# First block's weight loads regrouped over three issuing engines in a fused MLP forward and backward kernel

## The chip, the cores and the metric

The kernel runs on one core of one Trainium2 chip. The metric is the device time of one execution in microseconds, the median of several executions: 271.76 us before the change (three runs, 271.73 to 272.64). A core has a matrix engine (TensorE, PE in the profile, with weight loads listed as PEld), three engines for elementwise work (VectorE or DVE, ScalarE or ACT, GpSimd or POOL) and SyncE (SP), which here only issues transfers. Transfers are carried out by 16 DMA engines, which all queues of the core share. SP, ACT and POOL each have a queue of their own; an issuing instruction occupies its engine for some tenths of a microsecond up to several microseconds, and the data land later.

## The reference

A two-layer MLP with the tanh form of GELU, and its gradients, in bf16:

```python
B, S, D, F = 1, 2048, 448, 1792
h = jnp.einsum("bsd,df->bsf", x, w1) + b1
h = jax.nn.gelu(h, approximate=True)
out = jnp.einsum("bsf,fd->bsd", h, w2) + b2
# outputs: out and the gradients of x, w1, b1, w2, b2 for a given grad_out
```

## The kernel before, in words

The 2048 rows are worked in four blocks of 512 (`NB`, `SB`); the block that is worked first holds rows 512 to 1023. Inside a block the 1792 columns of the hidden layer are worked in seven pairs of 128-column tiles (`NPAIR`), in the order of `FP = [1, 2, 3, 4, 5, 6, 0]`. So pair 0 of a block reads columns 256 to 511 of w1, pair 1 columns 512 to 767, pair 2 columns 768 to 1023, pair 3 columns 1024 to 1279, and pair 6 columns 0 to 255.

For each pair the order, written out by hand under a manual schedule, is:

- `pe_u_fulls` (line 216): u = x·w1 with three matmuls of 128 rows of w1 (`w1_f`) per tile.
- `pe_tails` (line 237): the last 64 rows. 448 is three times 128 plus 64, and the 64 left-over rows of w1 stand in a tile of their own, `wt1` (the profile calls it wt). The left-over half of q, read from `w2T`, is worked beside it on the other 64 rows of the array. The two halves are issued alternately: u, q, u, q.
- `pe_q_fulls` (line 273): q = grad_out·w2ᵀ, from the transposed weight `w2T` and the transposed gradient `gT`.
- `copy_u` (line 311, with one line 313 on DVE), `act_gelu` (317), `act_square` (320), `act_tanh` (329) on ACT; `dve_cubic`, `dve_gate` and `dve_gh` (324 to 343) on DVE. They make `hT`, the activation, and `ghT`, the gradient before the first layer.
- `pieces` (line 372): the matmuls of the second layer, first with `w2_sb` and `hT`, and from pair 6 on with `w1T_sb` and `ghT` for the gradient of x.

u runs two pairs ahead of q. The numbers in brackets below, u(3) or q(1), count pairs through all blocks, and `pieces` behind q(1) needs hT(1).

In the first block all weights arrive from memory while the matmuls already run. SP issues nearly all of these loads in one order, written out at lines 142 to 168; ACT issues the first piece of w1, and POOL the bias b1. `load_w1` (lines 121 and 122) issues two transfers, the 384 full rows of a column range into `w1_f` and the 64 left-over rows of the same range into `wt1`. `load_w2` (line 125) loads row tiles of w2 into `w2_sb`. `load_w2T` (lines 129 to 133) loads w2 transposed, for columns 0 to 255 in two transposes and one 2 KB copy of 64 by 16 single elements (line 133). `load_g` (line 114) and `load_x` (line 104) are transposing loads of one block. Line 167 loads the whole of w1 transposed into `w1T_sb`. Plain and transposing loads go through the same SP queue in that order. In the compiled program the loads of SP and ACT take eight landing counters in turn, so that a load waits for the landing of the eighth load before it.

At the start 42 dummy matmuls (line 172) run on PE until x arrives. After the four blocks come the weight gradients (lines 662, 673, 694), which work on data held or reloaded by then.

Of the kernel before, what the change touches and what calls it, by code (L numbers as in the profile page):

```python
# [19 lines left out]
def kernel(  # L20
# [15 lines left out]
    nc = tc.nc  # L36
    P = 128
    B, S, D = x.shape
    F = w1.shape[1]
    assert (B, S, D, F) == (1, 2048, 448, 1792)  # L40
    NS = S // P
    NF = F // P
    KF = D // P
    DL = D - KF * P
    SB = 512
# [8 lines left out]
    ROW0 = [SB, 2 * SB, 3 * SB, 0]  # L54
# [4 lines left out]
    x2 = x.rearrange("b s d -> (b s) d")  # L59
# [21 lines left out]
    w2T = const.tile([P, KF + 1, F], BF16, name="w2T")  # L81
# [13 lines left out]
    xT, gT = {}, {}  # L95

    def wide(src, r0, n, shift):
        return bass.AP(src.tensor, src.offset + r0 * D - shift, [[D, n], [1, (KF + 1) * P]])
# [11 lines left out]
    def load_g(b):  # L110
        t = blk.tile([P, KF + 1, SB], BF16, name="gT", tag="gT")
        r0 = ROW0[b]
        if b in WIDE:
            nc.sync.dma_start_transpose(out=t[:], in_=wide(g2, r0, SB, DL))  # L114
        else:
            nc.sync.dma_start_transpose(out=t[:, 1:KF + 1, :], in_=g2[r0:r0 + SB, DL:D])
            nc.sync.dma_start_transpose(out=t[:, 0, :], in_=g2[r0:r0 + SB, 0:P])
        gT[b] = t

    def load_w1(eng, f0, f1):  # L120
        eng.dma_start(out=w1_f[:, :, f0:f1], in_=w1[0:KF * P, f0:f1].rearrange("(kt p) f -> p kt f", p=P))  # L121
        eng.dma_start(out=wt1[0:DL, f0:f1], in_=w1[KF * P:D, f0:f1])  # L122

    def load_w2(eng, t0, t1):
        eng.dma_start(out=w2_sb[:, t0:t1, :], in_=w2[t0 * P:t1 * P, :].rearrange("(ft p) d -> p ft d", p=P))  # L125

    def load_w2T(f0, f1):
        if f0 > 0:
            nc.sync.dma_start_transpose(out=w2T[:, :, f0:f1], in_=wide(w2, f0, f1 - f0, DL))  # L129
        else:  # L130
            nc.sync.dma_start_transpose(out=w2T[:, :, 16:f1], in_=wide(w2, 16, f1 - 16, DL))
            nc.sync.dma_start_transpose(out=w2T[:, 1:KF + 1, 0:16], in_=w2[0:16, DL:D])
            nc.sync.dma_start(out=w2T[DL:P, 0, 0:16], in_=w2[0:16, 0:DL].rearrange("f d -> d f"))

    nc.vector.memset(zero[:], 0.0)
    nc.gpsimd.memset(b1_rows[:], 0.0)
# [2 lines left out]
    nc.gpsimd.dma_start(out=b1_rows[0:NF, :], in_=b1.rearrange("(ft p) -> ft p", p=P))  # L139
    xT[0] = blk.tile([P, KF + 1, SB], BF16, name="xT", tag="xT")  # L140
    halves = [slice(0, SB // 2), slice(SB // 2, SB)]
    nc.sync.dma_start_transpose(out=xT[0][:, :, halves[0]], in_=wide(x2, ROW0[0], SB // 2, 0))
    load_w1(nc.scalar, 256, 512)
    nc.sync.dma_start_transpose(out=xT[0][:, :, halves[1]], in_=wide(x2, ROW0[0] + SB // 2, SB // 2, 0))
    warm = stg.tile([P, 1], F32, name="warm", tag="warm", bufs=1)
    nc.scalar.activation(out=warm[:], in_=zero[:, 0:1], func=ACT.Gelu_apprx_tanh)
    load_w1(nc.sync, 512, 768)
    load_w1(nc.sync, 768, 1024)
    load_w2(nc.sync, 2, 4)
    load_g(0)  # L150
    load_w2T(256, 512)
    load_w2(nc.sync, 4, 6)
    load_w1(nc.sync, 1024, 1280)
    load_w2T(512, 768)
    load_w2(nc.sync, 6, 8)
    load_w1(nc.sync, 1280, 1536)
    load_w2T(768, 1280)
    load_w2(nc.sync, 8, 12)
    load_w1(nc.sync, 1536, F)
    load_w1(nc.sync, 0, 256)  # L160
    load_w2(nc.sync, 12, NF)
    load_w2(nc.sync, 0, 2)
    load_w2T(1280, F)
    nc.sync.dma_start(out=b2_bc[:], in_=b2.rearrange("(o d) -> o d", o=1).to_broadcast((P, D)))
    load_x(1)
    load_w2T(0, 256)
# [257 lines left out]
    loads = {6: ("x", 2), 8: ("g", 2), 10: ("x", 3), 11: ("g", 3)}  # L424
# [44 lines left out]
    for i in range(1, NSINGLE):  # L469
        f = i + LEAD  # L470
# [271 lines left out]
```

## Time and profile before

| what | value |
|---|---|
| median of three runs | 271.76 us |
| the profiled execution: its own time | 272.33 us |
| its span, first to last instruction | 270.5 us |
| PE busy in the span | 263.7 us (97%) |
| DVE / ACT / POOL busy | 176.1 / 139.3 / 39.7 us |
| first matmul on real data | 5.64 us |
| w1T_sb: issued, landed | 34.54 us, 46.01 us |
| granted TensorE clock | 1.000 |

The span is counted from the first instruction on; 1.8 us of the execution's own time lie around it, and that execution is 0.57 us above the median of the runs. PE is busy nearly all the time, so that time can only be won or lost where PE stands still. It does so in a few places, which the list of waits and the timeline of PE give one by one. In the DMA part of the page the queue q1 is SP's, q10 ACT's and q0 POOL's; q8 and q14 are transfers of instructions. "Us to landing" counts from the start of the issuing instruction to the landing of the data.

### The profile page before, as it was taken

The numbers are of one execution on the slowest core, as the hardware profiler recorded it, in microseconds if no ns is written. First come the engines' busy times: TensorE is split into PE (matmuls) and PEld (weight loads), VectorE is DVE, ScalarE is ACT, GpSimd is POOL, SyncE is SP. The second block draws the span as 40 slices with busy tenths as digits, with TensorE's granted clock in tenths as the row PEclk, the third lists the DMA queues.
The fourth block names the chain that finished last, engine by engine and source line by source line (L and its number), as shares of the span: only waits on it lengthen the run. The fifth ranks groups of instructions, "written<-read, shape, count | busy, mean of one in ns | idle before, by whom it ended". The sixth has DMA issues, their size and how long they took to land.

```text
span 270.5 us, 4721 instructions
## 1 busy us (share of the span) xinstructions
PE 263.7 (97%) x1941; PEld 148.0 (55%) x1948; DVE 176.1 (65%) x208; ACT 139.3 (51%) x163; POOL 39.7 (15%) x50
## 2 busy tenths in 40 slices
PE   8999998999999999999999999999999999999995
PEld 7334343444445665555457888874444665555554
DVE  1689999799999779696798930309999992000000
ACT  2898899689995867968676520012111211111111
POOL 1000004011002020110202021221510007900000
PEclk9999999999999999999999999999999999999999
DMA  7999989999999995162642439999311111999851
GB/s 161 207 186 252 180 168 186 252 261 183 250 257 218 266 210 130 61 166 58 168 101 93 78 56 249 368 242 271 92 40 39 41 29 45 195 224 227 202 126 34
DMA packets 112965, 44.44 MB, mean 164 GB/s; under 512 B 92032, under 2 KB 111824, under 8 KB 112944
## 3 DMA queue, kind: packets, MB, share of 16 engines
q1 hardware_dynamic: 106352, 36.43, 63.2%
q0 software_dynamic: 1824, 4.27, 5.2%
q10 hardware_dynamic: 4768, 3.44, 4.1%
q8 instruction: 15, 0.25, 0.4%
q14 instruction: 6, 0.05, 0.1%
HBM read 7.23 MB, written 14.23 MB: 79 GB/s over the span
## 4 chain that ended last, share of the span: by engine, by line
PE 82%; SPq 12%; DMA 4%; issue 1%; ACT 0%
PE ps L237 23%; PE ps_v L694 16%; PE ps_w L662 13%; PE pq L237 9%; PE pu L237 8%; DMA w1T_sb<-in_w_dram 4%; PE ps L372 4%; SPq L129 4%; PE pu L216 3%; PE pq L273 2%; PE ps_w L673 2%; SPq L125 1%; SPq L104 1%; SPq L121 1%; SPq L122 1%; SPq L114 1%
## 5 line engine op out<-in xcount | busy, mean ns | idle before, releaser
L311 ACT ACTIVATE U<-pu,b1T 128x512 bf16<-128x512 f32 x55 | 33.9, 687 | 20.3 <-PE pu L237 20.1
L343 DVE SCALAR_TENSOR_TENSOR ghT<-Z,pq 128x1024 bf16<-128x1024 bf16 x28 | 33.9, 1221 | 14.2 <-PE pq L237 11.5
L386 POOL DMA_DIRECT2D out_dram<-st x32 | 19.1, 602 | 161.4 <-ACT st L383 107.6
L694 PE MATMUL ps_v<-g_nat,h_nat 128*128 128x448 bf16 (+1 forms) x240 | 42.6, 340 | 0.0
L237 PE MATMUL pq<-gT,w2T 64*128 64x512 bf16 x242 | 36.2, 376 | 0.6 <-DMA w2T<-in_w_dram 0.5
L662 PE MATMUL ps_w<-gh_nat,x_nat 128*128 128x512 bf16 (+1 forms) x192 | 36.5, 352 | 0.0
L237 PE MATMUL ps<-w1T_sb,ghT 64*128 64x448 bf16 x336 | 33.9, 349 | 0.0
L694 PEld LDWEIGHTS <-h_nat 128*128 128x128 bf16 x240 | 23.3, 98 | 19.3 <-DMA out_dram<-st 0.3
L237 PE MATMUL ps<-w_sb,hT 64*128 64x448 bf16 x336 | 33.7, 349 | 0.0
L329 ACT ACTIVATE Z<-Z 128x2048 bf16<-128x2048 bf16 (+1 forms) x18 | 27.5, 1528 | 7.7 <-DVE Z L325 7.6
L648 DVE TENSOR_TENSOR acc<-acc,gh_nat 128x1792 f32<-128x1792 f32 x14 | 30.0, 2142 | 0.5
L662 PEld LDWEIGHTS <-x_nat 128*128 128x128 bf16 x192 | 18.7, 98 | 17.9 <-issue 0.4
L237 PEld LDWEIGHTS <-ghT 64*128 64x128 bf16 x336 | 23.5, 94 | 8.7
L320 ACT ACTIVATE A<-U 128x1024 bf16<-128x1024 bf16 (+1 forms) x19 | 27.7, 1457 | 0.7 <-DVE U L313 0.4
L317 ACT ACTIVATE hT<-U 128x1024 bf16<-128x1024 bf16 (+1 forms) x20 | 27.7, 1391 | 0.2
L237 PEld LDWEIGHTS <-hT 64*128 64x128 bf16 x336 | 20.4, 94 | 11.9
L697 ACT CAST st<-ps_v 128x448 bf16<-128x448 f32 (+1 forms) x15 | 7.6, 507 | 34.8 <-PE ps_v L694 34.8
L383 ACT CAST st<-ps 128x448 bf16<-128x448 f32 x20 | 9.8, 532 | 29.0 <-PE ps L237 27.6
L216 PE MATMUL pu<-xT,w_f 128*128 128x512 bf16 (+1 forms) x100 | 22.6, 366 | 0.6 <-DMA xT<-in_x_dram 0.4
L237 PEld LDWEIGHTS <-w2T 64*128 64x128 bf16 x248 | 18.0, 94 | 8.7 <-DMA w2T<-in_w_dram 1.1
L665 ACT CAST st<-ps_w 128x512 bf16<-128x512 f32 (+1 forms) x12 | 6.4, 533 | 28.9 <-PE ps_w L662 28.9
L237 PE MATMUL pu<-xT,w_f 64*128 64x512 bf16 x144 | 20.5, 376 | 0.0
(52 smaller groups left out, 256.0 us busy)
## 6 DMA issues: line engine op xcount, KB each, us to landing
hT_dram<-hT SPq DMA_DIRECT2D x28, 256.0 KB, 3.0
out_dram<-st POOLq DMA_DIRECT2D x32, 112.0 KB, 3.5
x_nat<-in_x_dram SPq DMA_DIRECT2D x1, 1792.0 KB, 9.5
g_nat<-in_grad_out_dram SPq DMA_DIRECT2D x1, 1792.0 KB, 14.4
out_dram<-st ACTq DMA_DIRECT2D x13, 112.0 KB, 3.4
w_f<-in_w_dram SPq DMA_DIRECT2D x6, 192.0 KB, 4.1
out_dram<-st ACTq DMA_DIRECT2D x9, 128.0 KB, 1.7
w_sb<-in_w_dram SPq DMA_DIRECT2D x5, 224.0 KB, 4.2
```

Of the source, the lines that this page charges most:

```text
L129: nc.sync.dma_start_transpose(out=w2T[:, :, f0:f1], in_=wide(w2, f0, f1 - f0, DL))
L216: nc.tensor.matmul(PU[f][a][:, rs], lhsT=w1_f[:, kt, cols(p, a)], rhs=xT[b][:, kt, rs], start=(kt == 0 and rs.start == 0), stop=False, ski ...
L237: mm = nc.tensor.matmul(ps, lhsT=w, rhs=m, start=start, stop=stop, tile_position=(hf.start, 0), skip_group_check=True)
L311: nc.scalar.activation(out=dst, in_=PU[f][a][:], func=ACT.Identity, bias=bias)
L317: nc.scalar.activation(out=rows(hT, r), in_=part(U4, r), func=ACT.Gelu_apprx_tanh)
L320: nc.scalar.activation(out=part(A4, ks), in_=part(U4, ks), func=ACT.Square, scale=math.sqrt(3.0 * GELU_A * GELU_C))
L329: nc.scalar.activation(out=z, in_=z, func=ACT.Tanh, scale=-1.0 / 3.0)
L343: nc.vector.scalar_tensor_tensor(out=rows(ghT, [k]), in0=part(Z4, [k]), scalar=1.0, in1=PQ[k][:], op0=ALU.add, op1=ALU.mult)
L386: nc.gpsimd.dma_start(out=(out2 if self.kind == "o" else gx2)[r:r + P, :], in_=st[:, 0:D])
L648: nc.vector.tensor_tensor(out=v, in0=in0, in1=gh_nat[:, b, :, j, :], op=ALU.add)
L662: nc.tensor.matmul(ps[:, 0:n * P], lhsT=x_nat[:, st_, kt * P:(kt + 1) * P], rhs=gh_nat[:, b, ft0:ft0 + n, j, :], start=(st_ == 0), stop=(s ...
L694: nc.tensor.matmul(ps[:, 0:w], lhsT=h_nat[ft][:, st_, :], rhs=g_nat[:, st_, h * w:(h + 1) * w], start=(st_ == 0), stop=(st_ == NS - 1))
```

## The change

The loads of the first block are regrouped; no computation changes, and PE and DVE execute the same instructions in the same order.

- `load_w1` no longer loads the left-over rows. A new function `load_rest` does, in three transfers in place of seven: columns 256 to 511 by ACT as before, columns 512 to 1791 in one load by ACT, and columns 0 to 255 by POOL.
- ACT issues three loads more: those left-over rows, columns 768 to 1023 of w1, and row tiles 2 and 3 of w2. A new function `behind` makes ACT, ahead of them, wait until the first transposing load of x has landed. They stand ahead of ACT's first work on u.
- POOL waits for the same landing and issues two small loads: the left-over rows of columns 0 to 255, and the 2 KB copy of single elements that stood at line 133.
- On SP tiles 4 to 7 of w2 come in one load in place of two, columns 1024 to 1535 of w1 in one in place of two, and tiles 8 to 13 of w2 in one in place of two. Columns 1024 to 1535 of w1 now come behind columns 512 to 767 of w2T, tiles 8 to 13 of w2 before the rest of w1, and tiles 0 and 1 of w2 behind the last large part of w2T. SP issues 56 transfers in all in place of 68.

```diff
 def load_w1(eng, f0, f1):
     eng.dma_start(out=w1_f[:, :, f0:f1], in_=w1[0:KF * P, f0:f1].rearrange("(kt p) f -> p kt f", p=P))
+
+def load_rest(eng, f0, f1):
     eng.dma_start(out=wt1[0:DL, f0:f1], in_=w1[KF * P:D, f0:f1])
+
+def behind(eng, transfer):
+    tc.add_manual_dep(eng.nop().ins, transfer.ins.name, mybir.DependencyInfo(mybir.DependencyClass.Sync, mybir.DependencyReason.DATA),
+                      reason="plain loads behind x")
...
-            nc.sync.dma_start(out=w2T[DL:P, 0, 0:16], in_=w2[0:16, 0:DL].rearrange("f d -> d f"))
...
-    nc.sync.dma_start_transpose(out=xT[0][:, :, halves[0]], in_=wide(x2, ROW0[0], SB // 2, 0))
+    first = nc.sync.dma_start_transpose(out=xT[0][:, :, halves[0]], in_=wide(x2, ROW0[0], SB // 2, 0))
     load_w1(nc.scalar, 256, 512)
+    load_rest(nc.scalar, 256, 512)
     nc.sync.dma_start_transpose(out=xT[0][:, :, halves[1]], in_=wide(x2, ROW0[0] + SB // 2, SB // 2, 0))
...
+    behind(nc.scalar, first)
+    load_rest(nc.scalar, 512, F)
+    load_w1(nc.scalar, 768, 1024)
+    load_w2(nc.scalar, 2, 4)
+    behind(nc.gpsimd, first)
+    load_rest(nc.gpsimd, 0, 256)
+    nc.gpsimd.dma_start(out=w2T[DL:P, 0, 0:16], in_=w2[0:16, 0:DL].rearrange("f d -> d f"))
     load_w1(nc.sync, 512, 768)
-    load_w1(nc.sync, 768, 1024)
-    load_w2(nc.sync, 2, 4)
     load_g(0)
     load_w2T(256, 512)
-    load_w2(nc.sync, 4, 6)
-    load_w1(nc.sync, 1024, 1280)
+    load_w2(nc.sync, 4, 8)
     load_w2T(512, 768)
-    load_w2(nc.sync, 6, 8)
-    load_w1(nc.sync, 1280, 1536)
+    load_w1(nc.sync, 1024, 1536)
     load_w2T(768, 1280)
-    load_w2(nc.sync, 8, 12)
+    load_w2(nc.sync, 8, NF)
     load_w1(nc.sync, 1536, F)
     load_w1(nc.sync, 0, 256)
-    load_w2(nc.sync, 12, NF)
+    load_w2T(1280, F)
     load_w2(nc.sync, 0, 2)
-    load_w2T(1280, F)
     nc.sync.dma_start(out=b2_bc[:], in_=b2.rearrange("(o d) -> o d", o=1).to_broadcast((P, D)))
```

## The prediction

> **What bounds the kernel now.** I read first the page's busy shares and PE's list of waits, then the chain that ended last between 30 and 52 us, then the timelines of PE, ACT, DVE and SP in the first 50 us, and last what the DMA engines moved in single stretches.
>
> ```profile
> PE 263.7 (97%) x1941; PEld 148.0 (55%) x1948; DVE 176.1 (65%) x208; ACT 139.3 (51%) x163; POOL 39.7 (15%) x50
> ...
> PE ps L372 <- DMA w1T_sb<-in_w_dram: 1.1, 1, 1.1
> PE pw L172 <- DVE zero L135: 1.0, 1, 1.0
> PE pq L237 <- DMA w2T<-in_w_dram: 0.5, 2, 0.3
> PE pu L216 <- DMA xT<-in_x_dram: 0.4, 1, 0.4
> ```
>
> PE is the bound. Its waits for data are three: for x at the start, for w2T twice, for w1T_sb once. The last three lie where the change works; x's own load and all that runs before it stay. What the waits cost is read from the timeline, against an iteration without a wait:
>
> ```profile
> 12.43 0.39 PE L237 MATMUL pu<-xT,wt 64*128 64x512 bf16 x1
> 13.05 0.39 PE L237 MATMUL pq<-gT,w2T 64*128 64x512 bf16 x1 [0.24 <-DMA w2T<-in_w_dram]
> ...
> 13.59 1.47 PE L273 MATMUL pq<-gT,w2T 128*128 128x512 bf16 x6
> 14.89 1.68 PE L372 MATMUL ps<-w_sb,hT 128*128 128x448 bf16 x8
> ...
> 23.21 0.39 PE L237 MATMUL pu<-xT,wt 64*128 64x512 bf16 x1
> 23.22 0.39 PE L237 MATMUL pq<-gT,w2T 64*128 64x512 bf16 x1
> ...
> 23.75 1.47 PE L273 MATMUL pq<-gT,w2T 128*128 128x512 bf16 x6
> 25.05 1.68 PE L372 MATMUL ps<-w_sb,hT 128*128 128x448 bf16 x8
> ```
>
> From the first tail to the q matmuls take 0.54 us at 23.21 and 1.16 us at 12.43: the first wait costs **0.62 us**. The same pair at 17.80 takes 1.21 us (the q matmuls' first record is missing; the others start at 19.23, one spacing of 0.22 later): the second costs **0.67**. For w1T_sb: q matmuls at 43.49, the next work would start 1.30 later, as 23.75 to 25.05, at 44.79; it starts at 46.05: **1.26**. Together 2.55 us, 0.9% of the time.
>
> The chain says what makes w1T_sb late: SP issues without a gap from 0.72 to 34.54, and then comes the load itself.
>
> ```profile
> 31.22 1.30 SPq L131
> ...
> 33.84 0.66 SPq L133
> 34.49 0.04 issue
> 34.54 11.47 DMA w1T_sb<-in_w_dram
> 46.01 0.05 issue
> 46.05 2.82 PE ps L372 x14
> ```
>
> And the DMA engines are not full ahead of it (columns: window, busy time per engine, clock, DMA share, GB/s):
>
> ```profile
> 34.50:36.50 2.00, 2.00 (x12) 0.98 (x11) 1.86 (x4) 2.00 (x3) 0.00 (x0) 1.00 0.28 6
> 36.50:41.00 4.50, 4.45 (x24) 1.88 (x24) 4.26 (x8) 3.97 (x5) 0.00 (x0) 1.00 1.40 242
> ```
>
> **What the change takes off SP.** Ahead of w1T_sb go six loads of left-over rows (0.56+0.50+0.49+0.50+0.49+0.49 = 3.03), w1 768 to 1023 (0.58), w2 2 to 3 (0.59), the copy of single elements (0.66), and by merging one w2 (0.58), one w1 (0.46) and one w2 (0.55); a merged load issues in the same time (448 KB took 0.59, 224 KB 0.58). With 12 gaps of 0.04 that is 6.95 us. How much earlier w1T_sb lands is bounded: at most 6.95, if issuing is all that holds it; at least the 2 us of 34.5 to 36.5, in which the engines moved 6 GB/s, since the copy of single elements no longer stands there. It lands between 39.1 and 44.0. PE wants it at 44.79, less what it gained before (0.9 at most): at 43.9. So I take the whole **-1.26**. Nothing on PE takes its place: the next load, gT of the second block, landed at 48.4 (41.99 + 6.4) and q(7) wants it at 50.11; it is issued behind w1T_sb and moves with it. ghT(6), ready at 47.6, is wanted at 50.1, or at 48.0 with all gains. From 52 us on PE runs without a wait over 0.1, so what is won at 46 stays.
>
> **w2T.** The part for q(0) landed at 12.97 (issued 9.37, 3.6 to landing). Four issues ahead of it go (0.56+0.58+0.50+0.59, gaps 0.16): issued at about 6.98, it lands at 10.6, or 12.4 with the 5.4 that gT took just ahead; wanted at 12.43. The first wait goes, **-0.62**. The part for q(1) was issued at 12.39, landed at 18.39, wanted at 17.80. It moves 3.4 us up (two issues more, 0.46+0.49): from 8.97, with 3.6 to 6.0, it lands at 12.6 to 15.0. **-0.67**.
>
> **What it adds.** ACT and POOL wait until x's first half has landed, 0.72 + 4.9 = 5.62. ACT then issues three loads: at 5.67 (0.56 like L122 on ACT), 6.28 (0.44), 6.77 (0.59), done at 7.40. Behind them on ACT stands copy_u(0), which started at 7.47, when PE had u(0): hidden by 0.07; if x's landing is told 0.3 later, ACT is 0.3 late, hT(0) comes at 10.8 in place of 10.53, and PE, which loads it at 10.60, waits 0.2. On POOL nothing stands behind until 42.85; its two loads serve q(6) and u(6), after 30 us, and cost nothing beyond 0.6 us of engine time (0.28 of 2 us), which now falls at 7 to 9.
>
> The three loads are wanted early: left-over rows for u(1) at 8.98, w1 for u(2) at 9.51, w2 at 10.82. Before, they were issued at 4.09, 4.70 and 5.86. Bounds from the nearest rows: the quickest landing is ACT's first w1, 2.7 us with the engines empty; the slowest of w1 and w2 are 5.4 and 5.3. The left-over rows' row on ACT is 3.8, beside x.
> - Low end: 8.4, 9.0, 9.5, no wait.
> - High end: 9.5, 11.7, 12.1: w1 is 2.2 us late, and the rest is hidden in that.
> - Value taken: w1 and w2 at this place and size took 3.4 and 3.6, giving 9.7 and 10.4; the rows are five times larger than any piece before and gT runs beside them, so I add 0.3 to 0.4. PE then waits 0.6 for w1 and nothing more. **+0.6**, ends 0 and 2.2.
>
> [...]
>
> **Taken back.** Once PE is faster, ACT and DVE are near. hT(1) is ready at 14.52 (ACT is busy without a gap from 10.44 to 22.65) and PE used it at 14.89; q(5) starts at 37.46 and overwrites what DVE has read by 37.25. I take **+0.2**, ends 0 and 0.4.
>
> **Sum.** -0.62 + 0.6 - 0.67 - 1.26 + 0.2 = -1.75. Against the profiled execution, 272.33, of which 1.83 lie around the span, that is 270.6; that execution is 0.57 above the median, so for the median 271.76 it is 270.0. I write 270.1.
>
> **The rivals.**
> - *ACT's loads come late.* One wait takes the place of another: with 1.2 to 2.2 us at w1 and w2 the sum is -1.15 to -0.15, so 270.6 to 271.6. For it: the DMA share from 5 to 10 us is 1.00 at 222 GB/s, so what is moved behind x competes with gT and w2T, and ACT's loads carry 580 KB. Against it: 3.4 to 3.8 us for all loads issued there before. It decides from 1.2 us on.
> - *Slower: w1 for u(3) behind a held transpose.* At 15.4 us an instruction transfer of 16 KB runs, and the w2T transpose in flight then took 6.0 us to land where the same shape took 3.6 before; likewise 43.0 to 44.5 us show 45 GB/s. Before, w1 1024 to 1279 was ahead of that transpose (landed 15.85, wanted 16.41). Now w1 1024 to 1535 is behind it. If the transpose has not landed when the instructions are fetched, it lands at 18.4, w1 some 1.0 later (0.66 for 224 KB behind it before, for 384 KB more), and u(3) waits 3.0 us: -1.75 + 3.0 = +1.25, 273.0. The point is whether the transpose lands before about 15.4; I work out 12.6 to 15.0.
> - *The engines, not the issuing, set w1T_sb.* If the 16 DMA engines were the limit to 46 us, w1T_sb would land when it did, all earlier gains would run into that wait, and the time stays at 271.8. For it: shares of 0.92 and more from 20 to 34.5 us. Against: 0.28 from 34.5 to 36.5. [...]
>
> **How the numbers follow.** Forecast 0.57, with its own range 269.6 (no wait for ACT's loads, the gain at 14.89 limited to 0.2 by hT(1): -2.13) to 270.4 (w1 1.2 late, nothing taken back: -1.35). Late loads on ACT 0.20. The held transpose 0.15, of which 0.11 end above +0.5%, the rest between. Engines as the limit 0.08. Half a per cent, 1.36 us, is about what a measurement of this kernel tells from no change. So faster 0.57, same 0.20 + 0.08 + 0.04 = 0.32, slower 0.11. The range of 8 in 10 goes from 269.6 to 272.2: it leaves out 0.06 below and 0.12 above.
>
> **What would show it.** After: SP issues w1T_sb between 27.6 and 32.5; PE's list has no wait for w1T_sb and at most a short one for w2T; new waits of some 0.6 us stand at u(1) or u(2), for wt or w_f, at 9 to 10 us; ACT's copy_u(0) starts at 7.5. Wrong would be: waits at u(2) or at the first w2 work over 1.2 us, a wait for w_f at u(3) near 16.5, or w1T_sb landing after 44.

## The result, and the profile after

The change makes the kernel slower, by half a per cent. The median of eight runs is **273.38 us** (272.9 to 273.93) against 271.75 of the kernel before (eight runs beside them, 271.01 to 272.64): a ratio of **1.0055 [1.0037, 1.0074]**. Forecast were 270.1 us, in a range of 269.6 to 272.2. The profiled execution took 273.01 us, with a span of 271.2. Line numbers after the change are higher by 8 (the u matmuls stand at L224, the tails at L245, the pieces at L380).

PE's waits for data after the change, from its list (us in total, times, longest):

```profile
PE pu L245 <- DMA wt<-in_w_dram: 0.9, 1, 0.9
PE ps L380 <- ACT Z L337: 0.7, 1, 0.7
PE pu L224 <- DMA w_f<-in_w_dram: 0.5, 1, 0.5
```

The waits for w2T and for w1T_sb are gone. Three others stand there, all of them in the first 19 us: for the left-over rows (wt), at the first work on w2, and for w1 (w_f). PE's timeline of the same execution shows their places. First the lines of the kernel before, then those after the change:

```profile
7.04 0.60 PE L237 MATMUL pu<-xT,wt 64*128 64x512 bf16 x2
...
8.98 0.60 PE L237 MATMUL pu<-xT,wt 64*128 64x512 bf16 x2
9.51 1.47 PE L216 MATMUL pu<-xT,w_f 128*128 128x512 bf16 x6
10.82 1.68 PE L372 MATMUL ps<-w_sb,hT 128*128 128x448 bf16 x8
```

```profile
5.43 2.07 PE L224 MATMUL pu<-xT,w_f 128*128 128x256 bf16 x12
7.43 0.60 PE L245 MATMUL pu<-xT,wt 64*128 64x512 bf16 x2
7.97 1.47 PE L224 MATMUL pu<-xT,w_f 128*128 128x512 bf16 x6
10.29 0.60 PE L245 MATMUL pu<-xT,wt 64*128 64x512 bf16 x2 [0.86 <-DMA wt<-in_w_dram]
10.83 1.47 PE L224 MATMUL pu<-xT,w_f 128*128 128x512 bf16 x6
13.05 1.67 PE L380 MATMUL ps<-w_sb,hT 128*128 128x448 bf16 x8 [0.75 <-ACT Z L337]
...
18.71 1.47 PE L224 MATMUL pu<-xT,w_f 128*128 128x512 bf16 x6 [0.54 <-DMA w_f<-in_w_dram]
...
46.66 2.81 PE L380 MATMUL ps<-w1T_sb,ghT 128*128 128x448 bf16 x14
```

Read against the spacing that the same steps have without a wait (six u matmuls 1.30 to 1.31, two tails 0.54, eight pieces 1.51):

| place | due | started | lost, us |
|---|---|---|---|
| tails of u(0), at half clock | 7.04, as before | 7.43 | 0.39 |
| tails of u(1), for wt | 9.27 | 10.29 | 1.02 |
| first work on w2 | 12.14 | 13.05 | 0.91 |
| u(3), for w1 1024 to 1535 | 18.01 | 18.71 | 0.70 |
| q(5), behind DVE | 39.10 | 39.33 | 0.23 |
| **sum** | | | **3.25** |
| won: w2T twice, w1T_sb | | | -2.55 |
| lost before the change too: tails of u(1) | 8.88 | 8.98 | -0.10 |
| **balance** | | | **+0.60** |

The balance, +0.60, is the distance between the two timelines from 46 us on (the work on w1T_sb starts at 46.66 after the change and at 46.05 before, and the weight gradients at 182.82 and 182.22). The line at 13.05 names ACT, but hT(0), which that work reads, was ready at 10.92. Tiles 2 and 3 of w2 landed at 13.0 (issued by ACT at 6.50, 6.5 to landing), so those were late. The first entry is no effect of the change: PE started at half clock, by the spacing of its matmuls, and the trace's record of the full clock (1.0) begins at 4.7 us in the execution of before (the spacing of the dummy matmuls falls there from 0.107 to 0.056) and at 6.6 in this one (the u matmuls, from 0.213 to 0.110). So the first u matmuls took 2.00 to the tails in place of 1.40, and they had started 0.21 earlier. The change is not what sets this: kernel 9, whose first loads are those of before, takes 1.93 for them, and kernel 2, whose first loads are those of after, 1.40.

The medians are 1.63 apart. The two profiled executions are 0.68 apart (0.60 in PE's timeline; the other 0.08 is not found there). To that come 0.58, by which the profiled execution of before lay above its median, and 0.37, by which that of after lies below its own. The last part comes from executions with a lower mean clock: four of the eight after the change have 0.992 or 0.993 and spans of 271.8 to 272.2, the other four 1.000 and 271.1 to 271.4.

At the end of the first block the change does what was forecast. In the chain before, SP issued w1T_sb at 34.54 and it took 11.47; SP's timeline and the windows after (window, length, busy time of PE, PEld, DVE, ACT, POOL, clock, DMA share, GB/s) show

```profile
32.48 6.31 SPq L175 DMA_TRANSPOSE w1T_sb<-in_w_dram  x1
```

```profile
32.50:41.70 9.20, 9.20 (x47) 3.75 (x45) 8.53 (x15) 8.14 (x10) 0.00 (x0) 1.00 0.99 205
```

It landed 9.2 us later, at 41.7, five before PE takes it up at 46.66, and the stretch of 6 GB/s is gone. At the beginning the chain now runs over a transposing load that holds SP, and over the load of w1 behind it:

```profile
9.09 3.78 SPq L135
12.91 5.76 DMA w_f<-in_w_dram
18.71 1.47 PE pu L224 x6
```

The issue of that w2T (columns 512 to 767, for q(1)) held SP for 3.78 us, where the same shape took 1.3 in the kernel before.

Where ACT's loads lost their time is seen in the DMA engines between 5.6 and 8.5 us. Columns are packets, MB and the share of 16 engines; then KB and us to landing for each issue (q1 is SP's queue, q10 ACT's):

```profile
q1 hardware_dynamic: 2249, 0.63, 112.7%
q10 hardware_dynamic: 4, 0.01, 1.0%
...
wt<-in_w_dram ACTq DMA_DIRECT2D x1, 160.0 KB, 4.9
...
gT<-in_grad_out_dram SPq DMA_TRANSPOSE x1, 8.9
```

ACT issued its three loads at 5.33, 5.85 and 6.50. Until 8.5 the engines worked on SP's queue, in which gT (issued at 4.10) is the transposing load; of ACT's queue they moved four packets. From 8.5 to 10.9 it is the reverse: q10 has 99.6% of the engines' time and q1 3.8%. gT, which took 5.4 us to land before, took 8.9. ACT's first two loads still landed ahead of it (10.2 and 10.75, against 13.0 for gT): they had not waited for its landing.

### The profile page after: what moved, and what is told of

Its sections match the earlier page's. It is cut to its first block, busy times and chain, and to the rows that moved or that the text cites. A ratio compares the mean times of both kernels' runs of the same rounds, so it can differ in the third digit from the quotient of the medians.

```text
span 271.2 us, 4722 instructions
## 1 busy us (share of the span) xinstructions
PE 264.8 (98%) x1948; PEld 148.5 (55%) x1948; DVE 175.9 (65%) x208; ACT 139.4 (51%) x163; POOL 41.1 (15%) x52
## 4 chain that ended last, share of the span: by engine, by line
PE 92%; SPq 4%; DMA 2%; issue 0%; ACT 0%
PE ps L245 23%; PE ps_v L702 16%; PE ps_w L670 13%; PE pu L245 9%; PE pq L245 9%; PE ps L380 7%; PE pu L224 6%; PE pq L281 6%; PE ps_w L681 2%; DMA w_f<-in_w_dram 2%; SPq L135 2%; SPq L114 1%; SPq L147 0%; SPq L150 0%; PE ps L384 0%; SPq L131 0%
## 5 line engine op out<-in xcount | busy, mean ns | idle before, releaser
L670 PE MATMUL ps_w<-gh_nat,x_nat 128*128 128x512 bf16 (+1 forms) x192 | 36.5, 353 | 0.0
L245 PE MATMUL pq<-gT,w2T 64*128 64x512 bf16 x242 | 36.2, 377 | 0.0
L245 PE MATMUL ps<-w1T_sb,ghT 64*128 64x448 bf16 x336 | 33.9, 349 | 0.0
L245 PE MATMUL ps<-w_sb,hT 64*128 64x448 bf16 x336 | 33.8, 349 | 0.0
L245 PEld LDWEIGHTS <-ghT 64*128 64x128 bf16 x336 | 23.4, 94 | 8.8
L245 PEld LDWEIGHTS <-hT 64*128 64x128 bf16 x336 | 20.5, 94 | 11.8
L391 ACT CAST st<-ps 128x448 bf16<-128x448 f32 x20 | 9.8, 532 | 30.4 <-PE ps L245 27.6
L224 PE MATMUL pu<-xT,w_f 128*128 128x512 bf16 (+1 forms) x102 | 23.5, 375 | 0.5 <-DMA w_f<-in_w_dram 0.5
L245 PEld LDWEIGHTS <-w2T 64*128 64x128 bf16 x248 | 18.1, 94 | 7.6
L245 PE MATMUL pu<-xT,w_f 64*128 64x512 bf16 x144 | 20.5, 376 | 0.0
```

Source lines behind the costliest of these rows:

```text
L224: nc.tensor.matmul(PU[f][a][:, rs], lhsT=w1_f[:, kt, cols(p, a)], rhs=xT[b][:, kt, rs], start=(kt == 0 and rs.start == 0), stop=False, ski ...
L245: mm = nc.tensor.matmul(ps, lhsT=w, rhs=m, start=start, stop=stop, tile_position=(hf.start, 0), skip_group_check=True)
L670: nc.tensor.matmul(ps[:, 0:n * P], lhsT=x_nat[:, st_, kt * P:(kt + 1) * P], rhs=gh_nat[:, b, ft0:ft0 + n, j, :], start=(st_ == 0), stop=(s ...
```

## The experiments

Two theories stood for the three new waits. *Behind the transposes*: the loads of another queue get no turn while SP's transposing load is carried out, whatever their size. *Bytes*: the regrouping brings more bytes forward than the engines can move by then, and it matters little who issues them. A third theory concerned the runs with a lower clock: *standstills* of PE near the start let its clock fall. Kernels 1 to 4, 5 to 8 and 9 to 12 ran on one chip each, with runs of the kernel before beside them (25, 27 and 28 runs; medians 271.68, 271.85 and 271.82). The dummy matmuls in some kernels add work on unused data.

**1. The three loads back on SP** (after, otherwise unchanged):

```diff
-    behind(nc.scalar, first)
-    load_rest(nc.scalar, 512, F)
-    load_w1(nc.scalar, 768, 1024)
-    load_w2(nc.scalar, 2, 4)
...
     load_w1(nc.sync, 512, 768)
+    load_rest(nc.sync, 512, F)
+    load_w1(nc.sync, 768, 1024)
+    load_w2(nc.sync, 2, 4)
     load_g(0)
```

> The changed kernel, but ACT's three loads (left-over rows from column 512, w1 768 to 1023, w2 tiles 2 and 3) go back to SP, ahead of gT, and nothing waits for x on ACT. Theory 'behind the transposes': issued by ACT after x has landed, the three loads got no turn on the DMA engines while gT's transposes ran (first packets 3.2 us after the issue), and PE's waits at u(1), about 1.0 us, and at the first work with w2, about 0.9 us, come from that. Then both waits go, gT and w2T are issued 1.7 us later, which costs 0 to 0.3 at q(0), the wait for w1 at u(3), 0.7 us, may stay: 1.4 to 1.9 us below the changed kernel, 271.5 to 272.0. Rival 'bytes': the engines are full from 5 to 12 us whatever the order, so the wait only moves from wt and w2 to w2T: within 0.4 of the changed kernel, 273.0 or more. Rival 'clock': the loss is the lower clock at the start or during the run; then nothing changes either.

Measured: 276.43 us, ratio 1.0196 [1.0148, 1.0245], from four runs that lie far apart (273.85 to 277.86). The waits at u(1) and w2 go, as the first theory says, but no time is won: PE then waits 1.3 for w2T at q(0) and 2.0 for w1 at u(3), and three of four runs have a mean clock of 0.987 to 0.994. The profiled one, at 0.999, has a span of 272.1. So their place behind gT, on another queue, made those loads late, and putting them ahead of it only makes SP's later loads late.

**2. w1 1024 to 1535 ahead of w2T 512 to 767** (after):

```diff
     load_w2(nc.sync, 4, 8)
-    load_w2T(512, 768)
     load_w1(nc.sync, 1024, 1536)
+    load_w2T(512, 768)
```

> The changed kernel, but columns 1024 to 1535 of w1 come ahead of the w2T transpose for q(1), as before the change. Theory: u(3)'s wait for w1, 0.7 us, comes from standing behind that transpose, whose issue took 3.8 us on SP; it goes, and w2T still lands before q(1) wants it: 0.5 to 0.8 us below the changed kernel, 272.6 to 272.9. Rival: the wait for w1 turns into a wait for w2T at q(1) of the same size, because the queue is late as a whole: no difference.

Measured: 272.04 us, ratio 1.0027 [1.0001, 1.0053]. The wait at u(3) is gone; those for wt (1.2) and for w1 at u(2) (0.7) stay. Runs with a clock of 0.998 and more have spans of 269.6 to 270.3, against 271.1 to 271.4 after the change: about 1.1 us, more than the wait of 0.70 that it removes. Three of ten have 0.992 to 0.994 and 271.7 to 272.2. The order of these two loads is a cause.

**3. ACT does not wait for x** (after, without `behind(nc.scalar, first)`):

> The changed kernel, but ACT's three loads don't wait for x; they are issued from 3.3 us on, behind ACT's first activation. Theory 'behind the transposes': they reach the engines before gT's transposes and land by 8 us; u(1)'s and w2's waits go, x's second half lands at most 0.6 us later: 1.0 to 1.9 us below the changed kernel, 271.5 to 272.4. Rival 'bytes': 580 KB ahead of or beside x's second half hold x by 1 to 2.5 us, and the first matmuls wait for that: no gain, 273 or more.

Measured: 273.29 us, ratio 1.0071 [1.0045, 1.0098]. ACT issues at 1.86, 2.45 and 3.27, wt, w1 and w2 are in time, and x is late: PE waits 1.6 for it in place of the rest. This is what *bytes* says: what was moved ahead of x cost what it saved (273.29 against 273.38 after the change). The wait for x is not what was wrong. The DMA engines between 4.25 and 7.25 us, while SP's second half of x is carried out (columns as above):

```profile
q1 hardware_dynamic: 1023, 0.26, 59.4%
q10 hardware_dynamic: 470, 0.30, 52.5%
```

So here ACT's loads are moved beside a transposing load of SP, 470 packets beside 1023; the first of them had been issued ahead of it (1.86 against 2.12). *Behind the transposes* doesn't hold in general.

**4. Only the copy of single elements moved to POOL** (before):

```diff
-            nc.sync.dma_start(out=w2T[DL:P, 0, 0:16], in_=w2[0:16, 0:DL].rearrange("f d -> d f"))
...
+    behind(nc.gpsimd, first)
+    nc.gpsimd.dma_start(out=w2T[DL:P, 0, 0:16], in_=w2[0:16, 0:DL].rearrange("f d -> d f"))
```

> The kernel before, but the 2 KB copy of single elements goes from SP to POOL, behind x's landing; nothing else. It tells what that copy alone held. Theory: it held SP's queue for 2 us and more ahead of w1T_sb; w1T_sb lands by 44.0 in place of 46.0, and PE's wait of 1.26 us goes: 270.3 to 270.8. Rival 'the engines are the limit': w1T_sb lands within 0.5 us of before, no difference: 271.4 to 272.0. A cost of the copy at its new place, at 6 to 11 us, would show as a longer wait for w2T at q(0).

Measured: 271.31 us, ratio 0.9985 [0.9963, 1.0006]. SP issues w1T_sb at 34.57, as before, and it lands at 44.8 in place of 46.0; PE's wait for it, 1.26 before, is gone. But the first w2T wait grew from 0.62 to 0.99, and the gain is smaller than expected; the interval doesn't exclude none at all. So the wait for w1T_sb needed only this 2 KB copy out of the way, none of the other regrouping.

**5. PE's two first standstills filled** (after; 16 dummy matmuls ahead of the tails of u(1), 12 ahead of the first work on w2):

```diff
     pe_u_fulls(1)
+    for w in range(16):
+        nc.tensor.matmul(pw[:, 0, 0:P], lhsT=zero[:], rhs=zero[:], start=True, stop=True)
     pe_tails([1], [])
...
     pe_u_fulls(2)
+    for w in range(12):
+        nc.tensor.matmul(pw[:, 0, 0:P], lhsT=zero[:], rhs=zero[:], start=True, stop=True)
     open_two(1, 2)
```

> The changed kernel with 28 more dummy matmuls on PE (zero times zero into a bank that nobody reads): 16 ahead of u(1)'s tails and 12 ahead of the first work with w2, the two places where PE waits about 0.9 us each. They leave the loads alone and only keep PE busy while it waits. In half of the changed kernel's runs the granted clock's mean is 0.992 to 0.994, and those runs have spans of 271.8 to 272.2 where the others have 271.1 to 271.4; no run of the kernel before is below 0.998. Theory 'clock': the waits themselves let the clock drop, so with PE busy no run is below 0.998, and the median falls to that of the undisturbed half, 272.9 to 273.2, or a little above where the dummies outlast the wait. Rival: the clock depends on something else (the chip, the power of the DMA traffic): again about half the runs below 0.995, median 273.4 or more.

Measured: 272.75 us, ratio 1.0027 [1.0011, 1.0043]. No run of ten has a clock below 0.998 (spans 270.5 to 271.6). The loads are as late as after the change, and the loss is about half as large; the two intervals overlap a little, so that half is a rough figure.

**6. Size of ACT's left-over rows** (after; ACT loads columns 512 to 767, 32 KB, POOL the rest):

```diff
-    load_rest(nc.scalar, 512, F)
+    load_rest(nc.scalar, 512, 768)
...
+    load_rest(nc.gpsimd, 768, F)
```

> The changed kernel, but ACT's left-over rows end at column 767, 32 KB in place of 160; POOL loads columns 768 to 1791 of them, 128 KB, ahead of its other two loads. It halves nothing that stands in front of ACT's loads, only their own size. Theory 'behind the transposes': ACT's first load still gets its first turn only when gT's transposes are through, so u(1) waits nearly as long, 0.6 to 1.0 us, and the time is within 0.5 of the changed kernel. Rival 'size': the 160 KB are what is late; u(1) waits under 0.3 and the time falls by 0.7 or more, below 272.7.

Measured: 272.74 us, ratio 1.0026 [1.0003, 1.0048]. 32 KB took 4.8 us to land where 160 KB took 4.9, and the tails of u(1) start at 10.28 where they started at 10.29. Its own size does not make this load late. (POOL's 128 KB were moved beside it, so the sum of the bytes is the same.) The wait at u(3) is 1.1. None of ten runs has a low clock here, though PE waits 0.7 at u(1) too.

**7. gT held until ACT's left-over rows have landed** (after):

```diff
+    rest = load_rest(nc.scalar, 512, F)
...
     load_w1(nc.sync, 512, 768)
+    behind(nc.sync, rest)
     load_g(0)
```

> The changed kernel, but SP holds gT's transpose until ACT's left-over rows have landed. ACT issues as before at 5.3 us. Theory 'behind the transposes': with no transposes on the engines the left-over rows land 2.5 to 3.5 us after their issue (4.9 in the changed kernel), at 8.0 to 8.9, and u(1)'s wait of 1.0 us goes; gT and w2T come 4 us later, and q(0) waits 1.5 to 3 us in its place, so the time is higher than the changed kernel's. Rival 'issued too late': ACT's issue at 5.3 alone makes them late; they land at 10 as before and u(1) waits as long.

Measured: 274.47 us, ratio 1.0113 [1.0076, 1.0149]. The landing of ACT's load and the costliest of the new waits of PE in this kernel:

```profile
wt<-in_w_dram ACTq DMA_DIRECT2D x1, 160.0 KB, 3.0
```

```profile
PE pu L225 <- DMA w_f<-in_w_dram: 1.7, 1, 1.7
```

Without gT ahead of it the same load lands in 3.0 us instead of 4.9 (issued at 5.44, there at 8.4), and u(1) waits for nothing. So gT, in flight ahead of it, is what held this load, by 1.9 us. Whether it did so because it transposes, or only because it was issued first, is not shown: another reading, that loads get their turn in the order of issue whatever the queue, fits the kernel after and kernels 1, 3, 6 and 7 as well, and no run had a plain load in gT's place. What SP issues later pays: u(3) starts at 19.87.

**8. Only late or small loads off SP, order kept** (before). POOL, behind x, loads the left-over rows of columns 1024 to 1791 and 0 to 255, SP one load of those of 512 to 1023, and the copy of single elements goes to POOL behind w2T 768 to 1279:

```diff
+    behind(nc.gpsimd, first)
+    load_rest(nc.gpsimd, 1024, F)
+    load_rest(nc.gpsimd, 0, 256)
     load_w1(nc.sync, 512, 768)
+    load_rest(nc.sync, 512, 1024)
     load_w1(nc.sync, 768, 1024)
...
-    load_w2T(768, 1280)
+    third = load_w2T(768, 1280)
+    behind(nc.gpsimd, third)
+    nc.gpsimd.dma_start(out=w2T[DL:P, 0, 0:16], in_=w2[0:16, 0:DL].rearrange("f d -> d f"))
```

> The kernel before with SP's order, and only small things taken off SP: the left-over rows of columns 512 to 1023 in one load on SP, the others (1024 to 1791 and 0 to 255) by POOL behind x's landing, and the copy of single elements by POOL behind the landing of w2T's columns 768 to 1279. SP issues seven transfers less ahead of w1T_sb. If issuing on SP, and not bytes, sets when w2T and w1T_sb come: w2T for q(0) is issued 0.5 us earlier and its wait of 0.6 falls to 0 to 0.3, the wait at q(1) goes, w1T_sb's wait of 1.26 goes: 269.6 to 270.4. If the bytes beside it set it: the wait at q(0) stays or grows, and the gain is that of the elements alone, 0.4 (271.3).

Measured: **270.71 us, ratio 0.9962 [0.9946, 0.9978]**, faster than both kernels. All ten runs have a clock of 0.999 or 1.000. The two longest waits of PE for data:

```profile
PE pu L228 <- DMA w_f<-in_w_dram: 0.6, 1, 0.6
PE pq L249 <- DMA w2T<-in_w_dram: 0.5, 1, 0.5
```

w1T_sb is issued at 32.15, as early as after the change, and costs no wait.

**9. Only SP's merges and order, from tile 4 of w2 on** (before):

```diff
-    load_w2(nc.sync, 4, 6)
-    load_w1(nc.sync, 1024, 1280)
+    load_w2(nc.sync, 4, 8)
     load_w2T(512, 768)
-    load_w2(nc.sync, 6, 8)
-    load_w1(nc.sync, 1280, 1536)
+    load_w1(nc.sync, 1024, 1536)
     load_w2T(768, 1280)
-    load_w2(nc.sync, 8, 12)
+    load_w2(nc.sync, 8, NF)
...
-    load_w2(nc.sync, 12, NF)
```

> The kernel before, with only the change's merges and its order on SP from w2 tile 4 on: w2 4 to 7 in one load, w1 1024 to 1535 in one and behind w2T's columns 512 to 767, the left-over rows of 1024 to 1535 in one behind it, w2 8 to 13 in one. ACT and POOL load as before. Theory 'order': w1 for u(3) now stands behind that transpose and a larger w2, and PE waits for it at u(3) by 0.7 to 3 us, as in the changed kernel (0.7) and with the loads given back to SP (2.0); the wait at q(1) goes, w1T_sb is issued 2 us earlier and its wait of 1.26 goes too: 271.5 to 273.5, not faster. Rival 'fewer pieces are good by themselves': no wait at u(3), 270 to 271.

Measured: 272.84 us, ratio 1.0053 [1.0027, 1.0079]. PE's timeline in this kernel:

```profile
16.17 1.67 PE L369 MATMUL ps<-w_sb,hT 128*128 128x448 bf16 x8 [0.77 <-ACT U L308]
...
19.55 1.47 PE L213 MATMUL pu<-xT,w_f 128*128 128x512 bf16 x6 [1.70 <-DMA w_f<-in_w_dram]
```

w1 for u(3) is issued at 13.10 behind w2T for q(1), lands 6.4 later, and is 1.7 us late. The work on tiles 4 and 5 of w2 was due at 15.23 and started at 16.17: the merged load of tiles 4 to 7 landed at 16.1 (11.18 and 4.9), where tiles 4 and 5 alone had landed at 14.5 in the kernel before. ACT's and POOL's loads play no part here. Three of ten runs have a clock of 0.993 or 0.994 (272.4 to 272.9 in span), the others have 270.5 to 271.7. This part of the change alone loses as much as the whole.

**10. As 8, POOL's left-over rows behind the landing of w2T 256 to 511:**

```diff
-    load_w2T(256, 512)
+    early = load_w2T(256, 512)
+    behind(nc.gpsimd, early)
+    load_rest(nc.gpsimd, 1024, F)
+    load_rest(nc.gpsimd, 0, 256)
```

> The faster kernel with the small loads on POOL, with its two loads of left-over rows waiting for w2T's columns 256 to 511 in place of x, so that they don't run beside gT and that transpose. If their 128 KB beside gT made q(0) wait (0.65 us there), that wait falls by 0.2 to 0.5 and the time by as much, to 270.2 to 270.5; if the left-over rows then come too late for u(3) (wanted at 18), a wait of 0.5 to 1 us for wt stands there and the time is 270.7 or more.

Measured: 270.87 us, ratio 0.9963 [0.9944, 0.9983]. The wait at q(0) nearly goes (it starts at 12.98, where 12.80 was due); one of 0.2 for wt at u(3) comes. The time is that of kernel 8: POOL's loads were not worth more care.

**11. A long standstill of PE at u(2)** (before; w1 768 to 1023 behind gT):

```diff
     load_w1(nc.sync, 512, 768)
-    load_w1(nc.sync, 768, 1024)
     load_w2(nc.sync, 2, 4)
     load_g(0)
+    load_w1(nc.sync, 768, 1024)
```

> The kernel before with one exchange on SP: w1 768 to 1023 and its left-over rows behind gT in place of ahead of it, so that PE stands still for some 2 us at u(2). It tells what one long wait of PE does to the clock. Theory 'a wait of PE lowers the clock': at least a third of the runs have a mean clock of 0.995 or less, as the changed kernel's, and those are 0.6 to 2 us longer than the others. Rival: the clock has to do with the changed kernel's DMA traffic: no run below 0.998.

Measured: 272.72 us, ratio 1.0039 [1.0009, 1.0069]. Five of ten runs have a clock of 0.993 or 0.994, with spans of 271.4 to 272.2, the other five 0.999 or 1.000, with 269.4 to 270.5. The profiled execution is one of the first kind. Its windows (the clock is the third column from the right) and its timeline:

```profile
10.00:12.00 2.00, 1.01 (x4) 0.46 (x5) 1.86 (x4) 2.00 (x4) 0.00 (x0) 0.88 0.95 162
12.00:14.00 2.00, 2.00 (x6) 0.76 (x5) 1.64 (x5) 2.00 (x3) 0.00 (x0) 0.50 1.06 276
14.00:16.00 2.00, 2.00 (x11) 0.62 (x8) 0.65 (x1) 0.29 (x1) 0.00 (x0) 0.77 1.87 183
```

```profile
10.99 2.27 PE L216 MATMUL pu<-xT,w_f 128*128 128x512 bf16 x6 [1.64 <-DMA w_f<-in_w_dram]
13.06 2.60 PE L372 MATMUL ps<-w_sb,hT 128*128 128x448 bf16 x8
```

After a standstill of 1.64 us the granted clock falls to 0.50, from 11.5 to 14.9 us; six u matmuls take 2.27 in place of 1.47, eight pieces 2.60 in place of 1.68.

**12. The same with the standstill filled** (36 dummy matmuls ahead of `pe_u_fulls(2)`, otherwise as 11):

```diff
     act_gelu([1])
+    for w in range(36):
+        nc.tensor.matmul(pw[:, 0, 0:P], lhsT=zero[:], rhs=zero[:], start=True, stop=True)
     pe_u_fulls(2)
```

> The same exchange, with 36 dummy matmuls on PE in the pause (2.0 us at full clock). Loads and waits for data are the same, only PE doesn't stand still. Theory: no run below 0.998, and the median is below that of the kernel with the open pause by 0.5 us or more, or equal to that kernel's undisturbed runs. Rival: the same share of low clocks as with the open pause.

Measured: 272.26 us, ratio 1.0007 [0.9994, 1.0019]; all ten runs have a clock of 1.000 and spans of 269.9 to 270.9. The data are late all the same, and the low clock does not come. So the standstill of 1.64 us is what made the clock fall in kernel 11 (0.993 or 0.994 in 5 of 10 runs), not the late load as such.

## Why the prediction was wrong, step by step

Three steps failed. ACT's loads cost 1.83 us more than before in place of 0.6; the wait for w1 at u(3), 0.70, had been put at nothing in the sum; and no term stood for a lower clock. The first alone would have left the time at about 271.3, inside the range.

**w1T_sb: right.** Issue between 27.6 and 32.5 and landing between 39.1 and 44.0 were forecast; 32.48 and 41.7 came, and the 1.26 us are won. But the issue came at the last moment of its range: 6.95 us of issuing went from SP, and it came to w1T_sb only 2.06 us earlier, because issues of transposing loads grew (3.78, 4.67 and 5.15 us in the first 26 us, where the same three took 1.31, 4.10 and 3.63 before). The other 2.27 us are a shorter way from issue to landing, 9.2 in place of 11.47. Kernel 4, which only moves the copy of single elements, lands w1T_sb 1.2 earlier; the 2 us that the prediction set as the least are more than this copy gives by itself. Where the rest comes from is open: with the copy still on SP the same way took 9.9 in kernel 9 and 10.5 in kernel 12.

**w2T: right in the account, wrong in the mechanism for q(0).** Both waits are gone. The part for q(0) was to land by 12.4; it was issued at 7.08, as forecast (6.98), but took 6.4 and landed at 13.5, 1.1 later than PE wanted it before. PE did not wait only because it was already late itself. Where it is not late, the wait is back: 1.3 in kernel 1, 0.6 in kernel 7. The part for q(1) landed at 15.7 (9.09 and 6.6), 0.7 past the upper bound, and still in time.

**What it adds: this step failed.** The cost of ACT's loads was taken as 0.6, w1 for u(2) alone, and it was 1.93: 1.02 for wt at u(1) and 0.91 at the first work on w2 (1.83 against the kernel before, which lost 0.10 at u(1)). The upper end given, 2.2, holds it. The value was chosen from 3.4 and 3.6, the landings of loads that SP had issued *ahead of* gT; ACT's come *behind* gT's issue, and took 4.9, 4.9 and 6.5. The 0.3 to 0.4 added for size was the wrong correction too: kernel 6 shows that 32 KB take as long as 160. The nearer row was ACT's own load of left-over rows beside x's transposes, 3.8, or the 5.4 of a load that shares the engines with transposes. The two queues did not share the engines at once: four packets of q10 were moved beside 2249 of q1 in 2.9 us. In kernel 3, where ACT had issued first, they did (470 packets beside 1023 in 3.0 us). Why ACT's packets came so late behind gT, the traces do not show.

**Copy_u(0): right in that it is not late.** ACT's issues ended at 7.00, ahead of PE's work on u(0); copy_u(0) began at 7.86, when the tails of u(0), 0.39 late by the start-up clock, were done. **Taken back: right**, 0.23 at q(5) for 0.2.

**The wait at u(3): put at nothing, close to the slower rival, by another way.** The rival said that w1 for u(3), moved behind w2T for q(1), would wait 3.0 us if that transpose had not landed by 15.4, when instructions are fetched. The transpose landed at 15.7, and the instructions came at 16.7, so its condition was not met; but u(3) waited 0.70. A window of the kernel after (columns as above):

```profile
16.60:18.50 1.90, 1.57 (x9) 0.59 (x6) 1.70 (x3) 1.90 (x3) 0.00 (x0) 1.00 0.45 25
```

From 14.0 to 16.6 the engines moved 316 GB/s, then 25 for 1.9 us, in which q8 carried its packet (16.7 to 17.7), and w1 landed at 18.67, right behind that. In kernel 9 such a stretch (22 GB/s) lies from 18.3 to 19.4, and w1 lands at 19.5; there the packet on q8 had ended at 17.5. In kernel 2, where w1 is ahead of the transpose, the engines move only 16 GB/s from 17 to 18 us and PE waits for nothing there. The place agrees with the rival, and so does a stretch in which hardly anything moves; it hit the end of w1's load and not the transpose ahead of it, so 3.0 us was too high a price. That the instructions cause the stretch is not shown. What neither the sum nor the rival had is that w1 was issued as late as 12.91: SP was held for 3.78 us by the issue ahead. Kernel 9, which regroups only SP's loads, shows 1.7 us there, 0.94 at w2, and the whole loss; kernel 2, which puts w1 ahead again, wins 1.1. The rival had a chance of 0.15, because the transpose was worked out to land at 12.6 to 15.0, as if it took in its new place what it took in the old.

**The engines as the limit** was half right. From 5 to 15 us it agrees with what happened: the DMA share there is 1.17 at 233 GB/s after the change, and 1.00 at 211 before, and in kernels 1, 3 and 7 each load that is helped makes another one late (PE then waits 2.0 us for w1, 1.6 for x and 1.7 for w1). The rival itself fails: w1T_sb did come 4.3 us earlier, and 2.06 of that is issuing time.

**What no step had: the clock.** Against the profiled execution the sum was -1.75, to 270.6; it came to 273.01. The gap of 2.43 is 1.23 for ACT's loads, 0.70 for u(3), 0.39 at the start-up clock, which is no effect of the change, 0.03 at q(5), and the 0.08 that PE's timeline does not show. For the medians come 0.37 from runs with a low clock, and 0.57, by which the execution of before lay above its own median and which was carried over to the forecast. Filling the standstills (kernel 5) brings the ratio from 1.0055 to 1.0027; the intervals overlap, but 0 of 10 runs have a low clock where 4 of 8 had. That a standstill lowers the clock is shown by kernels 11 (1.64 us, to 0.50) and 12. Why kernel 6, with waits of 0.7 and 1.1, has no such run is open, and so is what share of runs a given wait costs.

## What to carry to other kernels

While the matmuls already run and the engines are full, put the bytes in the order in which they are wanted; a merged load that saves 0.5 us of issuing brings forward bytes that nobody wants yet and holds back one that is wanted now (in kernel 9 tiles 4 and 5 of w2 landed at 16.1 in place of 14.5). A load that a second queue issues behind a large transposing load of the first should not be counted as sharing the engines at once; here its first packet came 3.1 us after its issue (5.33, 8.48). So give the second queue what is small or wanted late (kernel 8, 0.9962), and keep the rest where it was. Price a new wait on PE in the first microseconds above its length: a pause of 1.64 us cost some 1.9 more in the five of kernel 11's ten runs that have a lower clock.

## What the runs showed of the hardware that was not expected

- **A standstill of 1.64 us halved the granted clock for about 3.4 us** (kernel 11, 0.50 from 11.5 to 14.9). 5 of 10 runs with it have a mean clock of 0.993 or 0.994, 0 of 10 with it filled (kernel 12), and 1 of 80 runs of the kernel before (0.994). It cost some 1.9 us of span (kernel 11, 271.4 to 272.2 against 269.4 to 270.5).
- **At the start the clock rose at a different moment in the two profiled executions**: 4.7 us before (spacing of the dummy matmuls 0.107, then 0.056) and 6.6 after (u matmuls 0.213, then 0.110), with the same dummy matmuls ahead; that was worth 0.39 us here.
- **The issue of the same transposing load held SP for very different times.** The w2T for q(1) took 1.31 us in the kernel before, 3.78 after, 3.80 in kernel 6, but 1.23 in kernel 7 and 1.24 in kernel 9. After the change it stood behind 448 KB of w2 and ACT's 576 KB, and from 11.0 to 12.6 us the engines moved only 92 GB/s; what holds it no run separates.
- **Close to a transfer of instructions the engines moved little before and after the change**: 26 GB/s from 15.4 to 17.5 us before (packet on q8 from 15.2 to 16.7), 25 from 16.6 to 18.5 after (16.7 to 17.7), where w1 for u(3), close to landing, came at 18.67. That the one causes the other was not tried by a run. In kernel 9 the stretch began 0.8 us after the packet had ended, so they do not always coincide.
- **The 2 KB copy of 64 by 16 single elements on SP** delayed the next load there by 1.2 us (kernel 4). The engines moved 6 GB/s from 34.5 to 36.5 with it and 66 without. With it on POOL the ten runs lie within 271.01 to 271.69, where 25 runs of the kernel before on the same chip reach from 270.49 to 273.47; why it narrows them was not tried.
